# A job order that knows array shapes, one tail tile, an edge copy on VectorE and three FFN slices inside attention

## The chip, the cores and the metric

The kernel runs on one core of a Trainium2 chip. The metric is the device time of one execution in microseconds (us): the median of three runs of the kernel before is 946.44 us (945.19 to 946.77). The engines are named as the profile names them: PE (TensorE, with PEld for its weight loads), DVE (VectorE), ACT (ScalarE), POOL (GpSimd) and SP, the queue that issues DMAs.

## The reference

Windowed attention over 4 batches, 8 heads, 576 positions and head size 64, then two feed-forward layers (FFN) over the 2304 tokens. The weights arrive as 64-bit floats, which is why they have to be taken apart on the chip.

```
scores = (q @ k.T) / 8, plus slope[h] * -|i - j|;  kept where 0 <= i - j < 128
attn   = exp(scores - rowmax) / (rowsum + 1e-9);   x = (attn @ v) as 2304 x 512
h = x @ w_in;  g = h * sigmoid(1.702 * h);         x = g @ w_out     # 512 -> 2048 -> 512
h = x @ w_in2; g = h if h >= 1, 0 if h <= -1, else (h + 1)**2 / 4;   out = g @ w_out2
```

## The kernel before

**Attention** is cut into 16 units (a batch and a pair of heads). For each unit: SP loads q, k and v; PE transposes q and k in three steps (job q, line 339; step 2 is the tail of 64 positions) and DVE or ACT copies them out of PSUM (qe); PE forms scores in three groups (s, line 359); DVE adds the bias and takes the row maximum (t, line 370); ACT takes exp (x, line 378); DVE inverts the row sums (n1, n2); POOL scales (po, line 394); PE transposes the five blocks of probabilities (pt, line 406) and ACT copies all five out (pe, line 411); PE multiplies with v (pv, line 429), and ACT and DVE copy the two result tiles into the FFN's input xt (x0 and x1, lines 438 and 441).

**Weights.** The FFN has 16 slices of 128 hidden units. A slice comes as two raw halves (its part of w_in, then of w_out), each one DMA of 512 KB into one of two raw buffers. Each half passes seven steps: ACT Abs (line 197), four on DVE (199, 202, 205, 208), ACT cast to the high part (211), and the low part (213; on POOL within attention, on DVE later). A raw buffer is free after line 208.

**The order** of the attention part is written out by a planner: `jobs` lists every step with an engine, a cost, its needs, its buffers and a key, `in_order` walks the engines' queues with these costs, and the kernel issues the jobs as it returns them. The engines run in that order. SPLIT = 4 slices (8 halves) are converted among the attention jobs, and the first token block's input is split into high and low parts there (xh, xl).

**FFN.** Tokens go in 5 blocks of about 461. For a step i, stage h (12 matmuls of slice f, line 497) is followed by the activation (ACT 503, DVE 504, ACT 510, DVE 511) and, LAG = 2 steps later, by stage o (12 matmuls, line 558). A run is a block with a range of slices: block 0 with slices 0 to 7 (CUT = 8), block 1 with all 16, block 0 again with 8 to 15, then blocks 2 to 4. While the first runs work, the other 12 slices are converted, one every W1_PACE = 1.6 steps. After the first run its four sums are put aside: DVE copies each to `part` (line 522), which uses the two `ga` buffers of the activation, and SP writes it to DRAM (523). The second FFN is like the first, with blocks of 384. From line 475 on, Tile's own scheduler sets the order.

Of the kernel before, what the change touches and what calls it, by code (L numbers as in the profile page):

```python
# [30 lines left out]
KEYS = dict(dma=-3.04, v=-0.71, b=-0.56, q=-0.6, qe=-0.52, s=-0.5, t=-0.3, x=0.08, n=0.67, po=-0.49, pt=0.98, pe=0.72, pv=0.29, xe=0.54)  # L31
STEP, QSTEP, W_AT, W_STEP, XS_AT = 0.243, 0.09, 3.72, 1.69, 28.0
NM = 5
RUNS = [(0, 1), (2, 3), (4,)]
SHAPE_SWITCH, SLACK, AHEAD = 95, 150, 12
# [6 lines left out]
def jobs(nu, n_heads2, halves, chunks):  # L42
# [8 lines left out]
    for u in range(nu):  # L51
        def at(what, x=0.0):
            return u + KEYS[what] + x

# [6 lines left out]
        for c in range(3):  # L61
            occ, lat = (433, 631) if c < 2 else (114, 314)
            add(("q", u, c), "PE", occ, lat, at("q", c * QSTEP), [("dma", u), ("ident",)] + [("q", u, 0)] * (c > 0),
                [("a", (u, c))] + [("qk", u)] * (c == 0), [("raw", u)] * (c == 2), "128x128")
            occ, lat = (600, 725) if c < 2 else (157, 290)
            add(("qe", u, c), "DVE" if c < 2 else "ACT", occ, lat, at("qe", c * QSTEP), [("q", u, c)], gives=[("a", (u, c))])
        for g, ms in enumerate(RUNS):
            occ = (486, 648, 162)[g]
            banks = [("s", (u, g, e)) for e in range(len(query_groups(ms[0])))]
            add(("s", u, g), "PE", occ, occ + 195, at("s", g * STEP), [("qe", u, c) for c in range(g + 1)],  # L70
                banks + [("p", (u, m)) for m in ms], [("qk", u)] * (g == 2), "64x64")
            done = []
            for m in ms:
                for e, i, lo in query_groups(m):
                    k = {64: 0, 128: 1, 192: 2}[192 - lo]
                    x = g * STEP + 0.01 * (2 * m + e)
                    needs = [("s", u, g)] + [("b", u % n_heads2, e)]
                    add(("t", u, g, m, e), "DVE", (145, 212, 277)[k], (262, 329, 394)[k], at("t", x), needs,
                        gives=banks[e:e + 1] * (m == ms[-1]))
                    add(("x", u, g, m, e), "ACT", (343, 385, 439)[k], (472, 514, 568)[k], at("x", x), [("t", u, g, m, e)])  # L80
                    done.append(("x", u, g, m, e))
            add(("n1", u, g), "DVE", 73, 204, at("n", g * STEP), done)
            add(("n2", u, g), "DVE", 90, 340, at("n", g * STEP), [("n1", u, g)])
            for m in ms:
# [7 lines left out]
                add(("pt", u, m), "PE", 325 if wide else 217, 523 if wide else 415, at("pt", m * STEP / 2),
                    needs + [("pt", u, 0)] * (m > 0),
                    [("t", (u, m))] + [("pt", u)] * (m == 0), [("p", (u, m))], "128x128")
                add(("pe", u, m), "ACT", 365 if wide else 260, 510 if wide else 400, at("pe", m * STEP / 2),
                    [("pt", u, m)], gives=[("t", (u, m))])
        add(("pv", u), "PE", 1400, 1600, at("pv"), [("dmav", u)] + [("pe", u, m) for m in range(NM)],
            [("a", (u, 3)), ("a", (u, 4))], [("pt", u), ("v", u)], "64x64")
        add(("x0", u), "ACT", 306, 450, at("xe"), [("pv", u)], gives=[("a", (u, 3))])
        add(("x1", u), "DVE", 391, 500, at("xe"), [("pv", u)], gives=[("a", (u, 4))])  # L100
    for h in range(halves):
        key = W_AT + W_STEP * h
        add(("wd", h), "SP", 600, 4300, key - 1.0, takes=[("wraw", h)])
        for i, (eng, occ, lat) in enumerate((
                ("ACT", 590, 740), ("DVE", 343, 560), ("DVE", 343, 530), ("DVE", 604, 800), ("DVE", 600, 800),
# [542 lines left out]
```

## Time and profile before

| | |
|---|---|
| median of three runs | 946.44 us (945.19 to 946.77) |
| the profiled execution's own time | 945.34 us |
| its span, first to last instruction | 943.6 us |
| PE, PEld busy | 921.8 us (98%), 810.7 us (86%) |
| DVE, ACT, POOL busy | 546.8, 398.2, 76.7 us |
| granted TensorE clock | 1.000 over the whole span |
| chain that ended last | PE 85%, DVE 6%, DMA 4%, ACT 2% |

The profile's "busy" on PE includes the modelled ends of pipelined matmuls, so two starts of a row of the timeline tell more of PE's pace than the busy share. The clock column (granted clock 1.000, which is the level of 2.4 GHz) is the same in every stretch, so times of different stretches can be compared as they stand. In the timeline, the first column is the start and the second the duration, both in us; a bracket at the end gives the engine's idle time before the row and what ended it.

### The profile page before, as it was taken

How to read it: one execution, taken by the hardware profiler on the slowest of the kernel's cores; microseconds unless marked ns; L12 is line 12 of the kernel's file. 1: busy time of each engine (PE TensorE's matmuls, PEld its weight loads, DVE VectorE, ACT ScalarE, POOL GpSimd, SP SyncE). 2: the span in 40 equal slices, each digit the busy share in tenths (PEclk: the TensorE clock that was granted, in tenths of full speed). 3: DMA queues.
4: the chain of work that ended last, by engine and by line, in shares of the span. 5: the costliest groups of instructions: out<-in, count | busy, mean ns of one | idle time of the engine just before them, and what ended most of it. 6: DMA issues, size and time to landing. Idle time of an engine off the chain costs nothing.

```text
span 943.6 us, 15391 instructions
## 1 busy us (share of the span) xinstructions
PE 921.8 (98%) x5904; PEld 810.7 (86%) x5904; DVE 546.8 (58%) x1290; ACT 398.2 (42%) x948; POOL 76.7 (8%) x176
## 2 busy tenths in 40 slices
PE   7989989999999999999999999999999999999998
PEld 5667678788888989999888989899899998998997
DVE  6887988999334223322589899634434434344343
ACT  5988984454323213222355455422422323323322
POOL 4555640000000000000000000000000000000000
PEclk9999999999999999999999999999999999999999
DMA  5777524444200000000044244000000000000000
GB/s 131 163 171 181 156 81 130 151 126 145 66 1 1 1 1 1 1 1 0 1 134 134 91 133 134 35 1 1 34 0 1 34 1 1 34 1 1 34 1 33
DMA packets 83129, 55.31 MB, mean 59 GB/s; under 512 B 59120, under 2 KB 76784, under 8 KB 83056
## 3 DMA queue, kind: packets, MB, share of 16 engines
q1 hardware_dynamic: 82912, 54.21, 20.1%
q8 instruction: 46, 0.75, 0.3%
q14 instruction: 27, 0.22, 0.1%
q10 hardware_dynamic: 144, 0.13, 0.0%
HBM read 48.66 MB, written 5.66 MB: 58 GB/s over the span
## 4 chain that ended last, share of the span: by engine, by line
PE 85%; DVE 6%; DMA 4%; ACT 2%; SPq 1%; issue 1%; POOL 0%; ACTq 0%; DVEq 0%; POOLq 0%
PE ph L497 39%; PE o L560 21%; PE o L558 19%; PE ps_x L429 2%; DMA raw<-in_moe_w_in_dram 2%; PE ps_s L359 2%; DMA raw<-in_moe_w_out_dram 1%; PE ps_t L406 1%; PE ps_qk L339 1%; DVE x L208 1%; DVE x L205 1%; DVE p L370 1%; DMA qkraw<-in_k_dram 1%; DVE qk L345 1%; DMA sp<-part 1%
## 5 line engine op out<-in xcount | busy, mean ns | idle before, releaser
L497 PE MATMUL ph<-xs,w 128*128 128x384 f32 (+2 forms) x2112 | 431.2, 353 | 0.0
L497 PEld LDWEIGHTS ph<-xs,w 128*128 128x128 f32 x2112 | 385.2, 188 | 28.6
L558 PE MATMUL o<-gs,w 128*128 128x460 f32 (+1 forms) x960 | 214.5, 372 | 2.3 <-DVE part L522 1.8
L560 PE MATMUL o<-w,gs 128*128 128x512 f32 x864 | 215.8, 394 | 0.0
L558 PEld LDWEIGHTS o<-gs,w 128*128 128x128 f32 x960 | 180.2, 188 | 24.0 <-DVE part L522 2.8
L560 PEld LDWEIGHTS o<-w,gs 128*128 128x128 f32 x864 | 161.2, 188 | 30.0 <-ACT gs L510 0.3
L510 ACT CAST gs<-ph 128x384 fp32r<-128x384 f32 (+2 forms) x176 | 89.4, 508 | 164.3 <-DVE ph L508 111.9
L511 DVE TENSOR_TENSOR gs<-ph,gs 128x384 fp32r<-128x384 f32 (+2 forms) x176 | 104.3, 593 | 71.5 <-ACT gs L510 71.4
L507 DVE TENSOR_TENSOR ph<-ph,ga 128x384 f32<-128x384 f32 x96 | 54.2, 565 | 145.0 <-ACT ga L506 145.0
L504 DVE TENSOR_TENSOR ph<-ph,ga 128x460 f32<-128x460 f32 (+1 forms) x80 | 51.4, 643 | 125.0 <-ACT ga L503 124.9
L506 ACT ACTIVATE ga<-ph,half 128x384 f32<-128x384 f32 x96 | 55.8, 581 | 139.3 <-PE ph L497 133.6
L503 ACT ACTIVATE ga<-ph 128x460 f32<-128x460 f32 (+1 forms) x80 | 44.1, 553 | 138.9 <-PE ph L497 138.6
L394 POOL TENSOR_SCALAR p<-p,sm 128x192 f32<-128x192 f32 (+1 forms) x144 | 61.7, 447 | 41.1 <-DVE sm L370 12.8
L197 ACT ACTIVATE x<-raw 128x512 f32<-128x512 f32 x64 | 43.1, 675 | 47.7 <-DMA raw<-in_moe_w_out_dram 23.2
L378 ACT ACTIVATE p<-p,sm 128x192 f32<-128x192 f32 (+1 forms) x144 | 62.1, 438 | 0.0
L508 DVE SCALAR_TENSOR_TENSOR ph<-ga,ph 128x384 f32<-128x384 f32 x96 | 53.8, 561 | 2.8
L211 ACT CAST w<-x 128x512 fp32r<-128x512 f32 x64 | 39.5, 619 | 20.9 <-DVE x L208 19.7
L370 DVE CUSTOM_DVE_ANT_0 p<-ps_s,bias 128x192 f32<-128x192 f32 (+1 forms) x144 | 41.7, 331 | 9.0 <-PE ps_s L359 8.1
L205 DVE SCALAR_TENSOR_TENSOR x<-raw,x 128x512 int32<-128x512 int32 x64 | 44.0, 688 | 0.5
L208 DVE SCALAR_TENSOR_TENSOR x<-raw,x 128x512 int32<-128x512 int32 x64 | 43.8, 686 | 0.7
L406 PE MATMUL ps_t<-ident,p 128*128 128x128 f32 x208 | 36.7, 288 | 5.5 <-POOL p L394 3.9
L213 DVE TENSOR_TENSOR w<-x,w 128x512 fp32r<-128x512 f32 x56 | 38.3, 687 | 2.2 <-ACT w L211 0.6
(47 smaller groups left out, 468.3 us busy)
## 6 DMA issues: line engine op xcount, KB each, us to landing
raw<-in_moe_w_in_dram SPq DMA_DIRECT2D x32, 512.0 KB, 3.7
raw<-in_moe_w_out_dram SPq DMA_DIRECT2D x32, 512.0 KB, 3.5
out_dram<-ob SPq DMA_DIRECT2D x17, 256.0 KB, 2.0
vraw<-in_v_dram SPq DMA_DIRECT2D x32, 128.0 KB, 2.9
qkraw<-in_q_dram SPq DMA_DIRECT2D x30, 128.0 KB, 3.9
qkraw<-in_k_dram SPq DMA_DIRECT2D x30, 128.0 KB, 2.7
sp<-part SPq DMA_DIRECT2D x4, 231.0 KB, 4.3
xt<-sp SPq DMA_DIRECT2D x4, 231.0 KB, 2.9
```

Source lines behind the costliest of these rows:

```text
L205: nc.vector.scalar_tensor_tensor(out=x, in0=raw[:, :, 0], scalar=29, in1=x, op0=ALU.logical_shift_right, op1=ALU.bitwise_or)
L208: nc.vector.scalar_tensor_tensor(out=x, in0=raw[:, :, 1], scalar=SIGN_TOP, in1=x, op0=ALU.bitwise_and, op1=ALU.bitwise_or)
L378: nc.scalar.activation(x, x, AF.Exp, bias=sm[:, 0, a, e:e + 1], scale=-1.0, accum_out=sm[:, 1, a, e:e + 1])
L394: nc.gpsimd.tensor_scalar(out=x, in0=x, scalar1=st[u]["sm", g][:, 2, a, e:e + 1], scalar2=1.0, op0=ALU.mult, op1=ALU.mult)
L497: nc.tensor.matmul(ph, w[f][:, a, 0, c * P:(c + 1) * P], xs[r][c][:, b, :], start=(c == 0 and i == 0), stop=(c == KC - 1 and i == 2))
L506: nc.scalar.activation(a, ph, AF.Relu, scale=0.5, bias=half)
L507: nc.vector.tensor_tensor(out=ph, in0=ph, in1=a, op=ALU.max)
L508: nc.vector.scalar_tensor_tensor(out=ph, in0=a, scalar=1.0, in1=ph, op0=ALU.min, op1=ALU.mult)
L510: nc.scalar.copy(gs[:, 0, :], ph)
L511: act_last[0] = nc.vector.tensor_tensor(out=gs[:, 1, :], in0=ph, in1=f32(gs[:, 0, :]), op=ALU.subtract)
L558: nc.tensor.matmul(o[r][m][:, 0:n], w[f][:, a, 1, sl], gs[:, b, :], start=first, stop=last)
L560: nc.tensor.matmul(o[r][m], gs[:, b, sl], w[f][:, a, 1, :], start=first, stop=last)
```

## The change

- The planner's PE shapes are now "square" (128 x 128: q, pt, and the new h) and "half" (s, pv), with a cost of its own for each pair of neighbours (SWITCH), where before any change of shape cost 95. Costs of s and pv are raised, and every kind of job has new keys, for each step its own.
- The 64-row tails of q and k lie in one raw tile (q on partitions 0 to 63, k on 64 to 127), so that one 128 x 128 transpose takes the place of two of 64 rows.
- Of the two edge blocks of probabilities (m = 0 and 4), the copy of m = 4 goes to DVE; ACT keeps four of five.
- SPLIT = 5: ten halves are converted within attention. CUT = 5: the first run has slices 0 to 4, and the third 5 to 15. The conversion of the other 11 slices starts at step 2, one every 1.5 steps.
- Stage h of slices 0 to 2 for block 0 and its activation (jobs h, ga, gm, gc, gl) are part of the planner's order, in the PSUM banks of the scores. In `stage_h` these three steps then issue nothing. The sigmoid waits for the last unit's last exp.
- The four `part` copies go to ACT. The split of block 0's input is planned from chunk 3 to chunk 0.

```diff
-SPLIT = 4
-CUT = 8
+SPLIT = 5
+CUT = 5
+AHEAD_H = 3
 LAG = 2
-W1_PACE, W2_PACE = 1.6, 1.66
+W1_PACE, W2_PACE = 1.5, 1.66
...
-KEYS = dict(dma=-3.04, v=-0.71, b=-0.56, q=-0.6, qe=-0.52, s=-0.5, t=-0.3, x=0.08, n=0.67, po=-0.49, pt=0.98, pe=0.72, pv=0.29, xe=0.54)
+KEYS = dict(
+    dma=(14.11,), v=(17.92,), b=(-9.64,), q=(-5.39, -6.79, -5.67), qe=(-0.81, 1.92, 1.52), s=(-5.08, -4.22,
...
+EDGE = ("ACT", "DVE")
...
-SHAPE_SWITCH, SLACK, AHEAD = 95, 150, 12
+SWITCH = {("square", "square"): 57, ("square", "half"): 105, ("half", "square"): 140, ("half", "half"): 10}
+SLACK, AHEAD = 52, 12
...
+                eng = "ACT" if wide else EDGE[m > 0]
+                occ, lat = (365, 510) if wide else (260, 400) if eng == "ACT" else (391, 500)
+                add(("pe", u, m), eng, occ, lat, at("pe", m), [("pt", u, m)], gives=[("t", (u, m))])
...
+    for f in range(AHEAD_H):
+        key = KEYS["h"][0] + KEYS["h"][1] * f
+        add(("h", f), "PE", 2510, 2700, key, [("xl", c) for c in range(chunks)] + [("w6", 2 * f)], [("s", ("h", f))],
+            shape="square")
+        if f <= LAG:
+            last = [("x", nu - 1, g, m, e) for g, ms in enumerate(RUNS) for m in ms for e, _, _ in query_groups(m)]
+            needs = [("h", f)] + (last if f == 0 else [("ga", f - 1)])
+            add(("ga", f), "ACT", 450 + 1300 * (f == 0), 600 + 1300 * (f == 0), key + KEYS["h"][2], needs)
...
-                if j.shape and shape and j.shape != shape:
-                    t = max(t, clock[eng] + SHAPE_SWITCH)
+                if j.shape and shape:
+                    t = max(t, clock[eng] + SWITCH[shape, j.shape])
...
-            n = 256 if c < 2 else 64
-            for i in range(2):
-                for t in range(0, n, P):
-                    r = min(P, n)
-                    nc.tensor.transpose(
-                        ps[:, i, t:t + r], d["raw"][0:r, i, 2 * c + t // P].rearrange("p h d -> p (h d)"),
-                        ident[0:r, 0:r])
+            for i, t in [(i, t) for i in range(2) for t in range(2)] if c < 2 else [(0, 0)]:
+                x = d["raw"][:, 4 * i + 2 * c + t if c < 2 else 8]
+                nc.tensor.transpose(ps[:, i, t * P:(t + 1) * P], x.rearrange("p h d -> p (h d)"), ident)
...
+        def do_h(f):
+            h_psum[f] = ps_s.tile([P, 512], F32, tag="s", name="ph")[:, 0:B1[0]]
+            products_h(h_psum[f], w1[f], xs0)
+            ahead[f] = (h_psum[f], None)
...
+            if (which, r) == (1, 0) and f in ahead:
+                ph, gs = ahead[f]
+                if gs is not None:
+                    gt[r, f] = gs
+                    return
...
-                    nc.vector.tensor_copy(part, src[:, 0:n])
+                    nc.scalar.copy(part, src[:, 0:n])
...
-    W1_AT = {max(0, round((g - SPLIT) * W1_PACE)): g for g in range(SPLIT, NF)}
+    W1_AT = {LAG + round((g - SPLIT) * W1_PACE): g for g in range(SPLIT, NF)}
```

**Place 1: PE within attention.** In these rows `ps_qk` is a q or k transpose, `ps_s` a score, `ps_t` the transpose of a probability block (`p_105` to `p_114` are its ten buffers before) and `ps_x` the product with v; xN counts repeats. This is the kernel before, some four units in.

```order
L406 MATMUL ps_t<-ident,p_110 128x128 x2
L339 MATMUL ps_qk<-ident,qkraw 128x128 x4
L359 MATMUL ps_s<-qk 64x192 x2
L406 MATMUL ps_t<-ident,p_111 128x128 x3
L406 MATMUL ps_t<-ident,p_112 128x128 x3
L339 MATMUL ps_qk<-ident,qkraw 128x128 x4
L406 MATMUL ps_t<-ident,p_113 128x128 x3
L406 MATMUL ps_t<-ident,p_114 128x128 x2
L359 MATMUL ps_s<-qk 64x64 x2
L359 MATMUL ps_s<-qk 64x128 x2
L359 MATMUL ps_s<-qk 64x192 x4
L429 MATMUL ps_x<-pt,vraw 64x64 x32
```

And this is one unit of the changed kernel in the same part (its p buffers are `p_108` to `p_117`), from the product with v to the scores ahead of the next one.

```order
L472 MATMUL ps_x<-pt,vraw 64x64 x32
L401 MATMUL ps_s<-qk 64x192 x8
L448 MATMUL ps_t<-ident,p_113 128x128 x2
L448 MATMUL ps_t<-ident,p_111 128x128 x3
L381 MATMUL ps_qk<-ident,qkraw 128x128 x4
L448 MATMUL ps_t<-ident,p_114 128x128 x3
L381 MATMUL ps_qk<-ident,qkraw 128x128 x4
L448 MATMUL ps_t<-ident,p_115 128x128 x3
L381 MATMUL ps_qk<-ident,qkraw 128x128
L448 MATMUL ps_t<-ident,p_117 128x128 x2
L401 MATMUL ps_s<-qk 64x192 x2
L401 MATMUL ps_s<-qk 64x64 x2
```

Before, no two units have the same sequence, and scores stand among the transposes; now the sequence repeats unit after unit, with all transposes in one stretch, and the scores of a unit stand about two products with v ahead of its own transposes.

**Place 2: ACT where attention ends.** `ga_2761` and `gs_2760` are the activation of slice 3, `x_2730` and `x_2739` the two halves of slice 5, `x_2825` the first half of slice 6 (each reads a raw buffer that a DMA fills), and `xs_2767` to `xs_2776` the high parts of block 1's input. The changed kernel:

```order
L234 CAST w_2577<-x_2673 128x512
L220 ACTIVATE x_2730<-raw_2728 128x512
L265 ACTIVATE ga_2761<-ph_2747 128x462
L220 ACTIVATE x_2739<-raw_2737 128x512
L234 CAST w_2727<-x_2730 128x512
L575 CAST gs_2760<-ph_2747 128x462
L279 CAST xs_2767<-xt0_67 128x460
L279 CAST xs_2770<-xt1_68 128x460
L220 ACTIVATE x_2825<-raw_2823 128x512
L234 CAST w_2727<-x_2739 128x512
L279 CAST xs_2773<-xt2_69 128x460
L279 CAST xs_2776<-xt3_70 128x460
```

Block 1's input is now split right behind the attention, with three waits for weight DMAs among its casts; before, that split stands eight steps of the FFN in.

**Place 3: the four sums of the first run.** Before, their copies (`part_3068` to `part_3086`) stand in DVE's order:

```order
L208 SCALAR_TENSOR_TENSOR x_3037<-raw_3035,x_3037 128x512
L522 COPY part_3068<-o0_2727 128x462
L511 TENSOR_TENSOR gs_3058<-ph_3045,gs_3058 128x460
L522 COPY part_3074<-o1_2728 128x462
L213 TENSOR_TENSOR w_3025<-x_3037,w_3025 128x512
```

In the changed kernel they stand in ACT's:

```order
L587 COPY part_2917<-o0_2711 128x462
L575 CAST gs_2907<-ph_2894 128x460
L220 ACTIVATE x_2886<-raw_2884 128x512
L234 CAST w_2874<-x_2877 128x512
L587 COPY part_2923<-o1_2712 128x462
L587 COPY part_2929<-o2_2713 128x462
L234 CAST w_2874<-x_2886 128x512
L220 ACTIVATE x_2941<-raw_2939 128x512
L587 COPY part_2935<-o3_2714 128x462
L265 ACTIVATE ga_2972<-ph_2958 128x460
```

Between the first and the second copy ACT now has an Abs that reads a raw buffer and a cast that needs DVE's four steps; the third copy and the next sigmoid share the two `ga` buffers with the copies, as before.

## Rows read from the trace of the kernel before

**Rows 1.** Busy time by stretch; columns: window, length, busy by engine, clock, DMA.
```profile
0.00:131.54 131.54, 115.73 (x1969) 85.26 (x1969) 104.82 (x494) 111.13 (x421) 76.13 (x176) 1.00 0.63 149
139.20:200.00 60.80, 58.55 (x276) 51.43 (x275) 55.20 (x104) 30.71 (x57) 0.00 (x0) 1.00 0.43 133
200.00:943.60 743.60, 739.89 (x3627) 667.06 (x3625) 379.35 (x682) 250.47 (x462) 0.00 (x0) 1.00 0.11 36
```
**Rows 2.** PE's timeline, from three places within attention and from its end.
```profile
18.84 0.77 PE L359 MATMUL ps_s<-qk 64*64 64x64 f32 x16
19.54 1.81 PE L429 MATMUL ps_x<-pt,vraw 128*64 128x64 f32 x61
21.14 0.37 PE L359 MATMUL ps_s<-qk 64*64 64x192 f32 x1
...
85.72 1.43 PE L359 MATMUL ps_s<-qk 64*64 64x64 f32 x32
87.07 0.44 PE L406 MATMUL ps_t<-ident,p 128*128 128x128 f32 x2
...
110.65 0.60 PE L339 MATMUL ps_qk<-ident,qkraw 128*128 128x128 f32 x4
111.18 0.54 PE L359 MATMUL ps_s<-qk 64*64 64x192 f32 x4
111.66 0.87 PE L406 MATMUL ps_t<-ident,p 128*128 128x128 f32 x6
112.37 0.60 PE L339 MATMUL ps_qk<-ident,qkraw 128*128 128x128 f32 x4
...
129.72 1.89 PE L429 MATMUL ps_x<-pt,vraw 128*64 128x64 f32 x64
131.54 7.82 PE L497 MATMUL ph<-xs,w 128*128 128x462 f32 x36
139.20 2.64 PE L558 MATMUL o<-gs,w 128*128 128x462 f32 x12
```
**Rows 3.** The chain that ended last, at 59 and at 68 us: start, us, what.
```profile
59.34 4.28 DMA raw<-in_moe_w_in_dram
...
68.88 4.36 DMA raw<-in_moe_w_out_dram
```
**Rows 4.** ACT busy from 10 us to the end of attention.
```profile
10.00:131.54 121.54, 109.69 (x420) 1.00 0.64 153
```
**Rows 5.** ACT's groups by shape within attention: busy us, mean ns, idle before.
```profile
L411 ACT COPY pt<-ps_t 128x256 f32<-128x256 f32 x32 | 12.0, 374 | 0.9 <-PE ps_t L406 0.7
...
L197 ACT ACTIVATE x<-raw 128x512 f32<-128x512 f32 x9 | 6.1, 678 | 3.0 <-DMA raw<-in_moe_w_in_dram 2.2 <-DMA raw<-in_moe_w_out_dram 0.7
...
L211 ACT CAST w<-x 128x512 fp32r<-128x512 f32 x8 | 5.0, 620 | 0.0
```
**Rows 6.** Timeline of ACT and DVE where attention ends.
```profile
131.65 0.43 ACT L438 COPY xt<-ps_x 128x320 f32<-128x320 f32 x1 [0.21 <-PE ps_x L429]
...
133.09 0.41 DVE L441 COPY xt<-ps_x 128x256 f32<-128x256 f32 x1
...
134.78 1.28 ACT L503 ACT_TABLE_LOAD   x1
136.07 0.56 ACT L503 ACTIVATE ga<-ph 128x462 f32<-128x462 f32 x1
```
**Rows 7.** SP's issues of the w_in halves of slices 5 and 15.
```profile
134.17 0.37 SPq L190 DMA_DIRECT2D raw<-in_moe_w_in_dram  x1
...
217.95 0.38 SPq L190 DMA_DIRECT2D raw<-in_moe_w_in_dram  x1
```
**Rows 8.** The first run's sums put aside: DVE's first and third copy.
```profile
179.76 0.63 DVE L522 COPY part<-o 128x462 f32<-128x462 f32 x1
...
184.77 0.64 DVE L522 COPY part<-o 128x462 f32<-128x462 f32 x1 [0.23 <-DMA sp<-part]
```
**Rows 9.** DMA issues from 134 to 240 us: count, size, median us to landing.
```profile
raw<-in_moe_w_in_dram SPq DMA_DIRECT2D x13, 512.0 KB, 3.7
...
sp<-part SPq DMA_DIRECT2D x4, 231.0 KB, 4.3
```

More of the change, by code (lines that the diff above doesn't have):

```diff
@@ L51, in jobs, with at @@
     for u in range(nu):
-        def at(what, x=0.0):
-            return u + KEYS[what] + x
+        def at(what, i=0, x=0.0):
+            return u + KEYS[what][i] + x
         n = 14 if u == 0 else 6
@@ L93, in jobs @@
                     needs + [("pt", u, 0)] * (m > 0),
[L94 to L99, printed above, removed]
@@ L100, in jobs @@
-        add(("x1", u), "DVE", 391, 500, at("xe"), [("pv", u)], gives=[("a", (u, 4))])
-    for h in range(halves):
[L102 to L105, printed above, removed]
-                ("ACT", 515, 730), ("POOL", 1254, 1400))):
-            add((f"w{i}", h), eng, occ, lat, key + 0.01 * i, [(f"w{i - 1}", h)] if i else [("wd", h)],
+                    [("t", (u, m))] + [("pt", u)] * (m == 0), [("p", (u, m))], "square")
@@ new lines, in jobs @@
+                eng = "ACT" if wide else EDGE[m > 0]
+                occ, lat = (365, 510) if wide else (260, 400) if eng == "ACT" else (391, 500)
+                add(("pe", u, m), eng, occ, lat, at("pe", m), [("pt", u, m)], gives=[("t", (u, m))])
+        add(("pv", u), "PE", 1600, 1840, at("pv"), [("dmav", u)] + [("pe", u, m) for m in range(NM)],
+            [("a", (u, 3)), ("a", (u, 4))], [("pt", u), ("v", u)], "half")
+        add(("x0", u), "ACT", 306, 450, at("xe", 0), [("pv", u)], gives=[("a", (u, 3))])
@@ L108, in jobs @@
+        add(("x1", u), "DVE", 391, 500, at("xe", 1), [("pv", u)], gives=[("a", (u, 4))])
+    for h in range(halves):
+        key = KEYS["half"][0] + KEYS["half"][1] * h
+        add(("wd", h), "SP", 600, 4300, key + KEYS["wd"][0], takes=[("wraw", h)])
+        for i, eng in enumerate(W_ENG):
+            occ, lat = W_COST[eng, i]
+            add((f"w{i}", h), eng, occ, lat, key + KEYS["w"][i], [(f"w{i - 1}", h)] if i else [("wd", h)],
                 [("wx", h)] * (i == 0), [("wraw", h)] * (i == 4) + [("wx", h)] * (i == 6))
@@ L230, in tile_window_attention_two_ffn, with products_h, sigmoid, new_g @@
     NX = max(B1 + B2)
+    g_p = ctx.enter_context(tc.tile_pool(name="g_p", bufs=2))
+    def products_h(ph, w, xs):
+        for c in range(KC):
+            for i, (a, b) in enumerate(((0, 0), (0, 1), (1, 0))):
+                nc.tensor.matmul(
+                    ph, w[:, a, 0, c * P:(c + 1) * P], xs[c][:, b, :],
+                    start=(c == 0 and i == 0), stop=(c == KC - 1 and i == 2))
+    def sigmoid(ph, n):
+        a = g_p.tile([P, 512], F32, tag="ga", name="ga")[:, 0:n]
+        nc.scalar.activation(a, ph, AF.Sigmoid, scale=1.702)
+        return a
+    def new_g(n):
+        return g_p.tile([P, 2, NX], F32R, tag="gs", name="gs", bufs=LAG + 1)[:, :, 0:n]
+    def low_g(gs, ph):
+        return nc.vector.tensor_tensor(out=gs[:, 1, :], in0=ph, in1=f32(gs[:, 0, :]), op=ALU.subtract)
     def split_block(t0, n):
@@ L240, in split_block @@
         return parts
+    ahead = {}
     with ExitStack() as actx:
@@ L304, in do_dma @@
             d = st[u]
[L305 removed]
+            d["raw"] = raw_p.tile([P, 9, 2, D], F32, tag="raw", name="qkraw")
             c0 = 2 if u == 0 else 0
@@ L410, in do_pe @@
             c = chunks_of(m)
-            nc.scalar.copy(d["pt"][:, 3 * m + c[0]:3 * m + c[-1] + 1, :], d["ps_t", m][:, c[0]:c[-1] + 1, :])
+            copy = nc.vector.tensor_copy if m in (0, NM - 1) and EDGE[m > 0] == "DVE" else nc.scalar.copy
+            copy(d["pt"][:, 3 * m + c[0]:3 * m + c[-1] + 1, :], d["ps_t", m][:, c[0]:c[-1] + 1, :])
         def do_pv(u):
```

97 lines of the change are left out of this document (58 added, 39 removed).

## The prediction

> **What bounds the kernel now.** I read the stretches first. From 200 us on PE is busy 739.89 of 743.60 us and has the same work after the change, so only what lies ahead can move [rows 1]. In the attention, up to 131.54 us, no engine is full: PE 115.7, ACT 111.1, DVE 104.8 [rows 1]. From 139.20, where stage o of slice 0 starts, to 200 PE loses 2.25 us, all near the end of the first run [rows 1, 8]. The granted clock is 1.00 throughout.
>
> Next PE's own pace. From the first product with v (19.54) to the last (129.72) are 15 units in 110.2 us, 7.35 us each [rows 2]. The pieces of a unit, from start to next start where nothing waits [rows 2]: two q steps 2 x 0.53 (110.65 to 111.18); 13 probability transposes at 0.71 / 6 = 0.118, so 1.54 (111.66 to 112.37); a tail transpose 0.12; the small score group 0.48 (111.18 to 111.66); the two large ones 1.35 (85.72 to 87.07); the product 1.60 (19.54 to 21.14). With a change of shape between scores and product (the product takes 1.82 into full-array work at 129.72, 1.60 into scores, so 0.2) that is 6.35 us. The last three units lack the q and s of units that no longer exist, about 3 x 3.0. So PE needs some 15 x 6.4 - 9 = 87 us of the 110, and waits about 20. The chain shows two of the causes: at 59.34 and 68.88 the attention stands behind weight DMAs of 4.28 and 4.36 us, because ACT's Abs of a half whose data had not landed holds everything behind it [rows 3].
>
> So the attention is bound by waits in orders that don't fit, not by an engine, and the rest by PE alone. The figure to work out is T, the time at which stage o of slice 0 starts: 139.20 before, behind three stages h of 7.66 us together (131.54 to 139.20) [rows 2].
>
> **The attention.** The new order repeats one sequence per unit. Scores stand two products ahead of their own transposes, some 12 us for a way through DVE, ACT and POOL that needs about half of it; the weight DMAs are issued early. The first product comes later: ahead of it now stand 13 more transposes (1.54), a unit's q (1.18) and two score groups (0.48 + 0.70), so 19.54 + 3.9 = 23.4. Then 15 x 6.35 - 9 + 7.66, since stages h of slices 0 to 2 stand where the missing units' work was: 94 us, last product at 117.4, its end 1.8 later. Stage o writes the banks of that product's results, so it waits for their copies, 0.43 on ACT behind a pause of 0.21 and 0.41 on DVE [rows 6], about 0.7: T = 119.9 if nothing else waits.
>
> ACT gives a second floor. After 10 us it works 109.69 of 121.54 us [rows 4]. It loses 16 edge copies of 0.374 (-6.0), gains Abs and cast of two more halves, 2 x (0.678 + 0.620) = 2.6 [rows 5], and the activation of three slices with the table load, 6 x 0.56 + 1.28 = 4.6 [rows 6]: 110.9, so 120.9 if it never idles, of which some 2.5 us (slice 4) come after T. If it idles the same 11.9 us as before, T is 130.3. DVE gains 16 copies of 0.41 (6.6 us, hidden only while DVE is not the bound), two halves and six activation steps on its 104.8, so it gets close too.
>
> T lies between 119.9 and 130.3. I take 123, nearer the floor: three of the twenty us of waits stay, because three engines over 90% busy leave no room for a late step, but the two visible causes go. The tail tile itself gives 16 x 0.12, about 2 us of PE, which is in these numbers; its DMAs keep their count. The three stages h cost nothing extra as long as the last three units have that hole.
>
> On the shapes, the rows say that scores take 0.70 us into a product (18.84 to 19.54), as if a change lay there, while the new cost table counts both as "half" at 0.01. The Trainium skill (TensorEngine Tiling (Array Packing), Tiling Modes) says that a change of tiling mode drains the array, and lists 128 x 64 and 64 x 64 as two modes; the product stands at 128*64 and the scores at 64*64 [rows 2], so by the rule, too, the planner misses one change per unit, 16 x 0.2 = 3 us that its order does not avoid. The trace agrees; without that change T would be 3 us lower, and the sum goes by the row.
>
> **The FFN from T on.** The same matmuls as before from 139.20 on, 804.4 us, but with other waits. Before they are 2.3 us. Now:
> - Block 1's input is split right behind the attention, and ACT must first pass three Abs that wait for weight DMAs; the third stands between the casts. If slice 5's first DMA goes out at T + 1.5, when slice 4 frees its buffer, landing (3.7 [rows 9]), Abs and DVE's steps bring slice 6's landing to about T + 12.7, and the third cast to T + 14.5; PE wants it at T + 13.8 (five stages of 2.55 and half of the next). With the low parts 1.0, bounds 0 and 4.
> - The first run's sums: before, DVE copied at 179.76 the first and at 184.77 the third, which had to wait for the first one's DMA of about 4.3 us, as both use two buffers [rows 8, 9]. ACT has the same two buffers, and between first and second copy an Abs and a cast that depend on DMA and DVE. PE needs all four banks for the next block. I take 3.4 instead of 2.3: bounds 1 (ACT copies at once) and 6 (a DMA and a half's DVE steps more).
> - The last slices: before, 83.8 us lay between the w_in issues of slices 5 and 15 [rows 7], 8.4 each, with DVE 91% busy, and PE needed slice 15 some 20 us later than it was ready. Now it is ready at T + 1.5 + 83.8 + 8 = T + 93.3 (8 is 3.7 to land, 0.68, 0.62 and DVE's steps), and its stage h comes after 35 stages of 2.55, at T + 89, plus the waits above, T + 94. No margin is left: 1.4, bounds 0 and 8. The split for the third run falls into the same busy stretch: 1.2, bounds 0 and 2.
>
> Together 7.0 against 2.3: +4.7. Later nothing differs: the conversion of the second FFN's weights is paced as before.
>
> **Sum**, against the profiled execution's 945.34: -(139.20 - 123.0) = -16.2, +4.7, so 933.8. The median of the runs lay 1.1 above the profiled one; I add it: 934.9. With the bounds of T and of the waits (T from 119.9 to 127, waits from +1 to +8) the likeliest case itself spans 928 to 942.
>
> **Rivals.**
> 1. The waits stay: the new order is full in PE, ACT and DVE at once, and each late step is handed on. ACT then idles as before, T = 130.3: 945.34 - 8.9 + 4.7 + 1.1 = 942.2; with the 20 us of PE's waits kept, T = 137 and 949. For it: ACT and DVE come near 100% in T = 123, and 16 DVE copies add to that. Against it: scores lead by two units, and the edge copies leave ACT. 15%.
> 2. Slower than before: conversion starves PE in the second run. Three slices are now loaded in steps 4, 5 and 6 in a row, beside the split and the put-aside sums, and ACT's order waits at each Abs. If a slice then takes 10.5 us instead of 8.4, slice 15 is ready at T + 114.5, 20 us after PE wants it: 934.9 + 19 = 954. It decides from about 9.7 us a slice on, where the late 13 us eat the gain. For it: DVE's 91%. Against it: 8.4 already contains a put-aside and a split. 5%.
> 3. The FFN's new waits don't come (ACT is less busy than DVE was there, and the spare steps before slices are needed cover them): T = 121, 945.34 - 18.2 + 0.5 + 1.1 = 928.7, or less. 10%.
>
> **How the numbers follow.** Forecast 70%, rivals 15, 5 and 10%. The range 928.5 to 942.5 leaves out the upper half of rival 1, rival 2 and the lower part of rival 3. What a measurement of this kernel can tell from no change is 0.2%, 1.9 us. Faster by more: the forecast, rival 3, most of rival 1 and a little of 2, 93%; within: 3%; slower: 4%.
>
> **What would show it.** In the changed profile: products with v 6.2 to 6.6 us apart without a break, no weight DMA on the chain before 115 us, three groups of 12 stage-h matmuls between the last three products; stage o of slice 0 at 120 to 127; then PE waits of some 1 us at block 1's first stage h, 2 to 4 around the part copies and 1 to 3 at slices 14 and 15, and none from the third run's second step on. T beyond 129 would show rival 1 right, PE waits on `w` of 10 us or more rival 2. I would be wrong altogether if the gain came from after 300 us, or if stage h shifted the products of the last units by its whole length.

## The result, and the profile after

The changed kernel takes 936.77 us (median of four runs, 935.74 to 937.98); the kernel before, beside it, 945.82. The ratio is 0.9907, 95% interval 0.9885 to 0.9929. The predicted 934.9 is 1.9 us below the measured time. A second series gave 938.46 and a ratio of 0.9916 (0.9901 to 0.9931). The profiled execution took 937.98 us, with a span of 936.2.

The stretches of the changed kernel, as in [rows 1] (window, length, busy PE, PEld, DVE, ACT, POOL, granted clock, DMA share, GB/s), split where stage o of slice 0 starts:

```profile
0.00:128.59 128.59, 111.84 (x1989) 91.02 (x1989) 108.62 (x516) 109.37 (x412) 78.16 (x176) 1.00 0.65 154
128.59:200.00 71.41, 69.68 (x323) 61.63 (x324) 63.61 (x115) 35.82 (x67) 2.78 (x2) 0.98 0.43 139
200.00:936.20 736.20, 730.72 (x3579) 657.37 (x3577) 372.58 (x671) 246.78 (x457) 0.00 (x0) 1.00 0.11 35
```

Stage o of slice 0 starts at T = 128.59 instead of 139.20 [rows 2]: 10.6 us earlier. From there to the end it is 807.6 us instead of 804.4, so 3.2 are given back: 945.34 - 10.6 + 3.2 is the measured 937.9. The clock is no longer 1.00 throughout.

PE's timeline of the changed kernel, which answers to [rows 2]: the first product and the twelfth, then the end of the attention, where the three stages h (L259, 12 matmuls each) stand between the last products:

```profile
23.89 1.81 PE L472 MATMUL ps_x<-pt,vraw 128*64 128x64 f32 x61
...
98.34 1.81 PE L472 MATMUL ps_x<-pt,vraw 128*64 128x64 f32 x61
...
109.20 2.77 PE L259 MATMUL ph<-xs,w 128*128 128x462 f32 x12
...
114.78 2.77 PE L259 MATMUL ph<-xs,w 128*128 128x462 f32 x12
...
120.47 2.77 PE L259 MATMUL ph<-xs,w 128*128 128x462 f32 x12
123.17 0.34 PE L472 MATMUL ps_x<-pt,vraw 128*64 128x64 f32 x4
124.01 1.76 PE L472 MATMUL ps_x<-pt,vraw 128*64 128x64 f32 x60 [0.51 <-ACT xt L481]
128.59 4.10 PE L623 MATMUL o<-gs,w 128*128 128x462 f32 x12 [2.81 <-DVE xt L484]
132.52 1.84 PE L259 MATMUL ph<-xs,w 128*128 128x462 f32 x8
```

Where nothing waits, products are 6.2 to 6.4 apart, but the eleven units from 23.89 to 98.34 average 6.77. The difference is in PE's waits from 14 us to the end of the attention (us in total, times, longest):

```profile
PE ps_qk L381 <- DMA qkraw<-in_k_dram: 6.3, 5, 1.8
PE o L623 <- DVE xt L484: 2.8, 1, 2.8
PE ps_x L472 <- ACT xt L481: 0.5, 1, 0.5
PE ps_t L448 <- ACT pt L454: 0.2, 1, 0.2
```

PE now waits for loads of k. SP, which issues all loads in order, goes at the same pace: from unit to unit its first load of q comes 6.75 us later (ten units lie between these two rows of its timeline).

```profile
21.11 1.07 SPq L359 DMA_DIRECT2D qkraw<-in_q_dram  x2
...
88.61 1.15 SPq L359 DMA_DIRECT2D qkraw<-in_q_dram  x2
```

At the seam, where the attention hands over to the FFN, the timeline of DVE, and under it that of POOL, in the changed kernel, while PE stands idle from 125.8 (124.01 + 1.76) on:

```profile
125.68 0.41 DVE L222 TENSOR_SCALAR x<-x 128x512 f32<-128x512 f32 x1
126.12 1.44 DVE L225 TENSOR_SCALAR x<-x 128x512 int32<-128x512 int32 x1
127.48 0.62 DVE L272 TENSOR_TENSOR gs<-ph,gs 128x462 fp32r<-128x462 f32 x1
128.03 0.41 DVE L484 COPY xt<-ps_x 128x256 f32<-128x256 f32 x1
```
```profile
126.01 1.26 POOL L236 TENSOR_TENSOR w<-x,w 128x512 fp32r<-128x512 f32 x1 [3.05 <-ACT w L234]
```

The copy x1 of the last unit (L484), whose PSUM bank stage o needs, stands behind two conversion steps of slice 4 and a step of the activation (L272), and one of the conversion steps took 1.44 us beside POOL's step instead of 0.43. PE's clock around this pause (window, length, PE busy, clock, DMA):

```profile
126.00:128.50 2.50, 0.00 (x0) 0.93 0.54 195
128.50:131.00 2.50, 2.41 (x6) 0.50 0.00 0
...
132.00:133.00 1.00, 1.00 (x7) 1.00 1.02 358
```

The first stage o runs at half clock (granted clock 0.50), 3.93 us (128.59 to 132.52) instead of some 2.55: 1.4 us. The waits after it, and SP's issues of the w_in halves of slices 5 and 15 (the row that answers to [rows 7]):

```profile
144.76 1.32 PE L259 MATMUL ph<-xs,w 128*128 128x460 f32 x5 [0.32 <-DVE xs L280]
157.97 2.60 PE L623 MATMUL o<-gs,w 128*128 128x460 f32 x10 [1.41 <-ACT part L587]
227.15 0.89 PE L259 MATMUL ph<-xs,w 128*128 128x462 f32 x3 [0.65 <-DVE xs L280]
228.30 1.95 PE L259 MATMUL ph<-xs,w 128*128 128x462 f32 x8 [0.26 <-DVE xs L280]
```
```profile
130.26 0.37 SPq L213 DMA_DIRECT2D raw<-in_moe_w_in_dram  x1
...
212.21 0.38 SPq L213 DMA_DIRECT2D raw<-in_moe_w_in_dram  x1
```

### The profile page after: what moved, and what is told of

Its sections match the earlier page's. It is cut to its first block, busy times and chain, and to the rows that moved or that the text cites. A ratio compares the mean times of both kernels' runs of the same rounds, so it can differ in the third digit from the quotient of the medians.

```text
span 936.2 us, 15327 instructions
## 1 busy us (share of the span) xinstructions
PE 912.2 (97%) x5888; PEld 810.0 (87%) x5888; DVE 544.8 (58%) x1300; ACT 392.0 (42%) x936; POOL 80.9 (9%) x178
## 4 chain that ended last, share of the span: by engine, by line
PE 71%; DMA 10%; DVE 8%; ACT 5%; SPq 3%; issue 2%; POOL 0%; ACTq 0%; DVEq 0%; POOLq 0%
PE ph L259 34%; PE o L625 21%; PE o L623 13%; DMA raw<-in_moe_w_in_dram 4%; DMA raw<-in_moe_w_out_dram 3%; DMA qkraw<-in_k_dram 2%; DVE x L228 2%; DVE x L231 2%; ACT x L220 2%; SPq L359 2%; ACT p L420 1%; PE ps_x L472 1%; DVE w L236 1%; DVE x L222 1%; DVE gs L272 1%
## 5 line engine op out<-in xcount | busy, mean ns | idle before, releaser
L259 PE MATMUL ph<-xs,w 128*128 128x384 f32 (+2 forms) x2112 | 432.3, 353 | 1.3 <-DVE xs L280 1.2
L259 PEld LDWEIGHTS ph<-xs,w 128*128 128x128 f32 x2112 | 384.2, 188 | 31.6 <-DVE xs L280 2.3
L272 DVE TENSOR_TENSOR gs<-ph,gs 128x384 fp32r<-128x384 f32 (+2 forms) x176 | 104.4, 593 | 71.6 <-ACT gs L575 71.4
L568 DVE TENSOR_TENSOR ph<-ph,ga 128x460 f32<-128x460 f32 (+1 forms) x77 | 49.5, 643 | 125.5 <-ACT ga L265 125.5
L228 DVE SCALAR_TENSOR_TENSOR x<-raw,x 128x512 int32<-128x512 int32 x64 | 45.6, 714 | 0.5
L231 DVE SCALAR_TENSOR_TENSOR x<-raw,x 128x512 int32<-128x512 int32 x64 | 44.7, 700 | 0.7
L381 PE MATMUL ps_qk<-ident,qkraw 128*128 128x128 f32 x144 | 26.3, 288 | 12.5 <-DMA qkraw<-in_k_dram 7.7
```

Of the source, the lines that this page charges most:

```text
L228: nc.vector.scalar_tensor_tensor(out=x, in0=raw[:, :, 0], scalar=29, in1=x, op0=ALU.logical_shift_right, op1=ALU.bitwise_or)
L231: nc.vector.scalar_tensor_tensor(out=x, in0=raw[:, :, 1], scalar=SIGN_TOP, in1=x, op0=ALU.bitwise_and, op1=ALU.bitwise_or)
L259: nc.tensor.matmul(ph, w[:, a, 0, c * P:(c + 1) * P], xs[c][:, b, :], start=(c == 0 and i == 0), stop=(c == KC - 1 and i == 2))
L272: return nc.vector.tensor_tensor(out=gs[:, 1, :], in0=ph, in1=f32(gs[:, 0, :]), op=ALU.subtract)
```

## The experiments

Each ratio is to the kernel before, timed in the same series (medians 945.10 to 945.82). T and the last column are of each kernel's profiled execution, and T alone says little: it was 128.59 and 130.53 in two profiles of the changed kernel. In the second one PE waited longer for a load of k, and ran at half clock behind it, in the middle of the attention (timeline; then window, length, PE busy, PEld, DVE, ACT, POOL, clock, DMA):

```profile
103.78 0.66 PE L381 MATMUL ps_qk<-ident,qkraw 128*128 128x128 f32 x2 [2.07 <-DMA qkraw<-in_k_dram]
...
104.00:106.50 2.50, 2.50 (x12) 2.17 (x11) 1.46 (x6) 0.48 (x1) 0.74 (x2) 0.50 0.69 158
```

The profiles of the order alone, of stage h outside and of the edge copies on ACT have such a half clock too, from 102.9 or 105.0 us on; the changed kernel's first profile and all others have none within the attention. No row of the table down to the fourth v buffer can be told from the changed kernel by its time; the interval of the x copies first still overlaps both of the changed kernel's.

| kernel | median us | ratio to before (interval) | T | span - T |
|---|---|---|---|---|
| before | 945.82 | | 139.20 | 804.4 |
| changed | 936.77 | 0.9907 (0.9885 to 0.9929) | 128.59 | 807.6 |
| changed, again | 938.46 | 0.9916 (0.9901 to 0.9931) | 130.53 | 808.8 |
| order alone | 936.61 | 0.9904 (0.9887 to 0.9920) | 130.13 | 805.0 |
| stage h outside | 936.98 | 0.9903 (0.9886 to 0.9920) | 130.58 | 807.3 |
| put-aside copies on DVE | 937.36 | 0.9913 (0.9895 to 0.9931) | 126.76 | 805.9 |
| edge copies on ACT | 936.15 | 0.9901 (0.9885 to 0.9918) | 128.59 | 808.9 |
| more shape changes | 937.41 | 0.9919 (0.9902 to 0.9936) | 128.28 | 807.4 |
| fourth v buffer | 937.92 | 0.9916 (0.9900 to 0.9933) | 127.15 | 808.3 |
| x copies first | 940.36 | 0.9942 (0.9925 to 0.9959) | 127.10 | 812.5 |
| both of these | 941.92 | 0.9959 (0.9940 to 0.9978) | 123.81 | 811.0 |
| x first, casts before slice 6 | 937.76 | 0.9919 (0.9905 to 0.9933) | 124.57 | 809.8 |
| and before half of slice 5 | 940.00 | 0.9944 (0.9929 to 0.9959) | 127.51 | 810.6 |
| and low parts on POOL | 949.02 | 1.0032 (1.0018 to 1.0046) | 125.52 | 819.0 |

**The order alone.** The new order stays, with the tail tile and the edge copy on DVE. After planning, jobs of slice 4 and of stage h are left out of the list, and the FFN is that of before (cut lines are marked by three dots):

```diff
-SPLIT = 5
-CUT = 5
+SPLIT = 4
+CUT = 8
...
-W1_PACE, W2_PACE = 1.5, 1.66
+W1_PACE, W2_PACE = 1.6, 1.66
...
+            for _, (what, *args) in in_order(jobs(NU, NP, 10, KC), CAPS):
+                later = what in ("h", "ga", "gm", "gc", "gl") or what[0] == "w" and args[-1] >= 2 * SPLIT
+                if not later:
+                    do[what](*args)
...
-                    nc.scalar.copy(part, src[:, 0:n])
+                    nc.vector.tensor_copy(part, src[:, 0:n])
...
-    W1_AT = {LAG + round((g - SPLIT) * W1_PACE): g for g in range(SPLIT, NF)}
+    W1_AT = {max(0, round((g - SPLIT) * W1_PACE)): g for g in range(SPLIT, NF)}
```

> The new order of attention, the tail tile and the edge copy stay; the FFN is that of before (four slices converted inside, first run to slice 7, steps at 1.6, put-aside copies on DVE, stage h outside). The order of the jobs that remain is the changed kernel's. Theory: the order and the tail tile carry the gain, since the new places of stage h, of slice 4 and of the cut only shift work between two places: the last product starts 2 to 6 us ahead of the changed kernel's 124.0, three stages h of 7.7 us follow, stage o starts at 127 to 130, the FFN takes 804 to 806, and the time is 934 to 938. Rival: the stages h inside fill holes that stay empty here; then the last product stays at 124, stage o starts at 133.5, and the time is 940 to 942.

936.61 us: the whole gain, from the order with its tail tile (the edge copy, taken back below, is worth nothing that shows). T is 130.13, 9.1 us ahead of before, and the FFN takes 805.0, close to the 804.4 of before. The expected way failed in part: the last product stayed at 123.81. The scheduler of the FFN's code put 15 of the 36 stage-h matmuls between the last products by itself:

```profile
115.87 0.69 PE L259 MATMUL ph<-xs,w 128*128 128x462 f32 x2
116.53 0.46 PE L259 MATMUL ph<-xs,w 128*128 128x462 f32 x1
117.08 1.93 PE L259 MATMUL ph<-xs,w 128*128 128x462 f32 x8
119.59 1.88 PE L472 MATMUL ps_x<-pt,vraw 128*64 128x64 f32 x64
121.92 1.08 PE L259 MATMUL ph<-xs,w 128*128 128x462 f32 x4
123.81 1.88 PE L472 MATMUL ps_x<-pt,vraw 128*64 128x64 f32 x64 [0.80 <-DVE xt L484]
125.62 4.67 PE L259 MATMUL ph<-xs,w 128*128 128x462 f32 x21
```

**Stage h outside**, all else as changed (the jobs h, ga, gm, gc, gl are skipped):

```diff
+                if what not in ("h", "ga", "gm", "gc", "gl"):
+                    do[what](*args)
```

> The three stages h of block 0 and their activation are taken out of the attention's order and run right behind it, all else in the same order. Theory of the prediction: they fill holes that the last units leave, so the last product stays near 123.2, its end at 125, then 7.7 us of stage h and the sigmoid with its table load: stage o at 133 or later, 4 to 5 us slower than with them inside (941). Rival: PE had no holes there, the last product moves forward by the whole 7.7 us to about 115.6, stage o starts at 125 to 128.6 and the time is the same or up to 3 us lower.

The rival holds: the time is the same. Here too 15 matmuls slipped in, and the last product started at 124.24, against 124.01 with all 36 inside. But this profile has the half clock at 105 us, and so it is better compared with the changed kernel's second one: there the last product starts at 125.78, 1.5 us later. So, by these two profiles, the attention's holes hide about 3 of the 4.5 us that the 21 other matmuls take. T gains nothing (130.58 and 130.53), because the pause of 2.80 us at the seam is missing when stages h stand there.

**Two more parts, undone.** The put-aside copies on DVE, and the last probability block's copy on ACT, each in its old place of the order:

```diff
-                    nc.scalar.copy(part, src[:, 0:n])
+                    nc.vector.tensor_copy(part, src[:, 0:n])
```

> Only the four put-aside copies go back to DVE. Theory: they wait for buffers, the third for the first one's DMA, on either engine, so PE waits 1 to 2.5 us there as now (1.4), and the time is within 1.5 us of the changed kernel (936.8). Rival: DVE, which converts the weights, is the bound up to 220 us; four copies of 0.63 more on it delay slice 15 and the split for the third run by 2.5 us, and the time rises by 2 to 3 us (939).

```diff
-            copy = nc.vector.tensor_copy if m in (0, NM - 1) and EDGE[m > 0] == "DVE" else nc.scalar.copy
+            copy = nc.scalar.copy
```

> Only the copy of the last probability block of each unit goes back from DVE to ACT, in the same place of the order. Theory of the prediction: ACT, 109.4 us busy of the 128.6 before stage o of slice 0, is a floor; with 6.0 us more it is at 115.4, its idle time of 19 us covers part, and stage o starts 2 to 4 us later: 939 to 940. Rival: PE and the loads set the pace in the attention, ACT has room, and the time changes by less than 1 us.

Neither changes the time. On DVE the four sums cost three pauses of 0.84, 0.96 and 0.62, on ACT one of 1.41. With the edges on ACT it works 112.84 us up to 128.59 instead of 109.37, and T is the same 128.59: ACT is no floor.

**More changes of shape** (PE's order alone):

```diff
+            for u in range(2, NU):
+                i = todo.index(("s", u, 1))
+                n = next(j for j in range(i + 1, len(todo)) if todo[j][0] in ("s", "pv", "h", "pt"))
+                if todo[n][0] == "pt":
+                    todo.insert(n, todo.pop(i))
```

> In PE's order alone, the second score group of a unit moves behind the two probability transposes and the q step that follow it, or behind the next transpose job: changes between full-array work and the half-array work (scores, products) go from 39 to 65 in the attention (81 before the change). Theory: the change gained its time in PE's busy time by avoiding such changes. PE was busy 115.7 us up to the end of the attention before and 104.2 after without the stages h, 11.5 less, of which 1.9 are the tail tile; 9.6 over 42 changes are 0.23 each. So 26 changes cost 6.0 us of PE and the time rises by 4 to 6 us, to 941 to 943. Rival: the time went down because waits went; then the 6 us of waits for k data take up the extra changes, and the time rises by less than 1.5 us.

The rival holds: 937.41, T 128.28. PE's waits for k data after 14 us are 0.18, 0.80, 0.26, 0.65 and 0.62, 2.5 us instead of 6.3. PE did more and waited less. So PE is not what sets the pace of a unit any more. The price of a change still shows in PE's own time: from 14 us to T, less PE's waits, it is 107.6 us here, and 104.2 to 105.6 in the eight profiles with 39 changes, stage h inside and no half clock in the attention. That makes 2.0 to 3.5 us for 26 changes, 0.08 to 0.13 each (an estimate), and not the 0.23 of the theory.

**A fourth v buffer:**

```diff
-        v_p = pool("v_p", CAPS["v"])
+        v_p = pool("v_p", CAPS["v"] + 1)
```

> Theory: PE's waits for k data in the attention (after 20 us: 0.57, 1.52, 1.59, 1.83 and 0.78, 6.3 us together) come from SP's queue: a load of v that waits for one of three v buffers holds the loads of q and k behind it; a unit takes SP 6.8 us, of which its issues alone are about 5.9. With a fourth v buffer and the same order these waits fall below 2 us, stage o of slice 0 starts near 124, and the time falls by about 4 to 5 us (932). Rival 1: SP is full by its issues, or the transfers themselves are slow: the waits stay at about 6 us and the time is the same. Rival 2: k comes earlier, but ACT or DVE is the next bound: the waits move to ps_t and ps_x, and the time falls by under 1.5 us.

No gain that can be told from the spread of T. The waits for k fell from 6.3 to 3.9 (3.5 to 8.0 us in the other kernels with this order), and SP, held less by v buffers, now waited for q and k buffers. Which of SP's issue time, the buffers and the transfers sets the 6.75 us is open.

**The x copies first**, and then with the fourth v buffer too ("both"):

```diff
+            for name, ahead_of in ((("x0", NU - 1), ("gc", 1)), (("x1", NU - 1), ("w1", 8))):
+                todo.remove(name)
+                todo.insert(todo.index(ahead_of), name)
```

> Theory: the pause of 2.81 us ahead of stage o of slice 0 comes from DVE's order, in which the copy x1 of the last unit stands behind two weight steps of slice 4, and the granted clock of 0.50 behind it comes from that pause. Then, with x0 and x1 of the last unit ahead of those steps, stage o starts at about 126.4 instead of 128.59 with a pause under 1 us, the clock stays near 1.00, the first stage o takes 2.6 us instead of 3.9, and the time falls by 3 to 4 us (933). Rival 1: the copy is only the last of several late things (the low part gl of slice 0, the copy on ACT), and the start stays past 128: no change. Rival 2: the start is earlier, but slice 4's conversion is now later and the splits and the last slices give half of it back: 935.

> Theory: the two causes are independent, so the gains add: 8 us, about 929, with stage o of slice 0 at 121 to 122. Rival: the conversion of the later slices (DVE and the two raw buffers) sets the end of the second run; then an earlier start turns into waits on w at slices 13 to 15 and at the split for the third run, and only 4 to 5 us remain (932).

The seam does what was expected, the time does not: 940.36. PE's timeline of the first:

```profile
127.10 2.77 PE L627 MATMUL o<-gs,w 128*128 128x462 f32 x12 [0.54 <-ACT xt L481]
...
144.76 0.75 PE L259 MATMUL ph<-xs,w 128*128 128x460 f32 x1 [4.82 <-ACT xs L279]
145.85 4.37 PE L259 MATMUL ph<-xs,w 128*128 128x460 f32 x11 [0.34 <-DVE xs L280]
...
163.29 2.51 PE L627 MATMUL o<-gs,w 128*128 128x460 f32 x6 [1.75 <-ACT part L591]
```

Pause and half clock at the seam are gone. But the FFN's code is ordered by a scheduler, which answered two moved copies with another order of ACT: the Abs of slice 6, which waits for a DMA, now stands ahead of all four casts of block 1's input and not of two, and the sigmoid of slice 3 (135.24 in the changed kernel) now stands behind the second Abs of slice 5, at 140.01. PE waits 4.82 us there and again runs at half clock behind it. With both edits T is 123.81, near the 123 of the prediction (121 to 122 was expected of this run), and the same pause (4.92) follows. That kernel's twelve runs go from 936.5 to 946.4, and the profile shows the lowest. The granted clock over the whole span is 0.996 in that run and 0.991 in the two slowest, so they ran longer at half clock; where isn't seen.

**The casts moved back**, with the x copies first: ahead of slice 6, and then ahead of the second half of slice 5 too (the second kernel's edit, in part; the first has only the condition on slice 6):

```diff
+            with tc.issue_after(last_cast[0].ins) if g == SPLIT + 1 else nullcontext():
+                load_weights(w1_in, w1_out, g, w1[g], (0,) if g == SPLIT else (0, 1))
+        if i == LAG + 1:
+            with tc.issue_after(last_cast[0].ins):
+                load_weights(w1_in, w1_out, SPLIT, w1[SPLIT], (1,))
```

> The copies x0 and x1 first, as in the first experiment, and ACT's steps of slice 6 behind the four casts of block 1's input. Theory: the first experiment lost at that split what it won at the seam, 4.8 us of pause and some 2 us of half clock behind it, because ACT's order of the FFN had changed with the moved copies and the Abs of slice 6 stood ahead of all four casts. Then that pause falls to 1 to 2 us, the clock stays near 1.00 there, and the time is 933 to 935. Rival: conversion is the bound up to 220 us; then slice 6 and all after it come later, and the time lost at the split appears as waits on w at slices 13 to 15 or at the split for the third run: 937 to 940.

> As the casts-ahead-of-slice-6 kernel, and the second half of slice 5 also behind the four casts of block 1's input, so that they no longer stand behind its Abs, which waited 2.7 us for a DMA. There the pause ahead of block 1 was 4.1 us, and the half clock behind it cost some 2.5 more. Theory: up to 220 us two things must end together, PE's steps and the conversion of eleven slices, which DVE (90% busy) paces at 7.7 to 8 us a slice. Then the pause falls to 1 to 2 us, but PE comes 4 to 6 us earlier to slices 13 to 15, whose weights come no earlier, and waits on w there: 935.5 to 937.5. Rival: the pauses and the clock were the loss, and conversion has slack: no waits on w over 1 us, and 931 to 933.

The first leaves a pause of 4.10, because the casts still stood behind an Abs of slice 5 and the steps of slice 3's activation. So the Abs of slice 6 made only about 0.7 of the 4.82, and my reading of the first experiment was wrong in the main. The second shortens the pause to 2.38, and PE's timeline shows where the rest goes:

```profile
142.69 0.47 PE L259 MATMUL ph<-xs,w 128*128 128x460 f32 x1 [2.38 <-ACT xs L279]
...
160.85 1.40 PE L629 MATMUL o<-gs,w 128*128 128x460 f32 x5 [2.30 <-ACT part L593]
162.04 4.18 PE L259 MATMUL ph<-xs,w 128*128 128x460 f32 x12
...
224.44 3.08 PE L259 MATMUL ph<-xs,w 128*128 128x460 f32 x12 [0.67 <-ACT w L234]
```

The put-aside sums cost 3.1 us (0.77 and 2.30) and a half clock, and after all of it PE still waits for the cast of slice 15. Of the waits on w only 1.1 us came (0.67 and, on PE's weight loads, 0.43), not the 4 to 6 that I expected, since PE lost the time before it got there. But there is no slack: from slice 5's first issue to slice 15's are 82 us in the changed kernel and 84 here.

**Low parts on POOL**, for the eleven slices of the FFN, on top of the kernel just described (940.00):

```diff
-            late.append(partial(convert, 6, raw, x, w, i, nc.vector))
+            late.append(partial(convert, 6, raw, x, w, i, nc.gpsimd if w_in is w1_in else nc.vector))
```

> The kernel before, with the low parts (L236) of slices 5 to 15 on POOL instead of DVE: 22 steps of 0.69 us leave DVE, 15 us of some 85. Theory 1, DVE paces the conversion: it gets faster by 1 us a slice, waits on w go, and the time is 930 to 933. Theory 2, from the seam, where a DVE step that ran beside POOL's 1.26 us took 1.44 instead of 0.43, 1.67 instead of 0.68: each POOL step costs DVE 0.5 to 1.0 us, as much as it takes off; the time stays within 1 us of the kernel without it or is up to 5 us longer.

949.02, which is 9.0 us more than without this edit and slower than before the change: theory 2, and more than its 5 us. Groups of DVE and POOL between 165 and 215 us (busy, mean ns), first without and then with the low parts on POOL:

```profile
L228 DVE SCALAR_TENSOR_TENSOR x<-raw,x 128x512 int32<-128x512 int32 x13 | 8.9, 687 | 0.2
...
L222 DVE TENSOR_SCALAR x<-x 128x512 f32<-128x512 f32 x12 | 5.1, 423 | 2.4 <-ACT x L220 2.4
```
```profile
L236 POOL TENSOR_TENSOR w<-x,w 128x512 fp32r<-128x512 f32 x12 | 16.6, 1380 | 33.6 <-ACT w L234 33.6
L228 DVE SCALAR_TENSOR_TENSOR x<-raw,x 128x512 int32<-128x512 int32 x12 | 16.0, 1335 | 0.3
...
L222 DVE TENSOR_SCALAR x<-x 128x512 f32<-128x512 f32 x12 | 7.6, 636 | 3.3 <-ACT x L220 3.2
```

A half loses a step of 0.686 us on DVE, and two others grow by 0.65 and 0.21: more than it saved. (The other two of its four steps stay as they were: L231 686 and 683, L225 423 and 427 ns.) Conversion of slices 5 to 15 takes 86.7 us (129.61 to 216.28), and PE then waits at slices 14 and 15 and at the third run's split.

**The changed kernel again:**

> The changed kernel itself, on the same chip as these, for their comparison. If the waits are those of its order, stage o of slice 0 starts at 126.5 to 129 again behind a pause of 2.8 us on the copy x1, with a clock of 0.50 behind it, waits for k data are 4 to 6.5 us, and the median is 936 to 938.

T was 130.53 and the median 938.46, both outside what was expected, behind the same pause (2.80) and half clock at the seam; the wait for k of 2.07 us and the half clock behind it, shown above, came on top.

## Why the prediction was right, and which steps were not

**The time, 934.9: 1.9 us too low, and that close by luck in part.** The sum is built on the profiled execution, forecast at 933.8 and measured at 937.98: T came 5.6 us later than forecast, and the FFN lost 1.5 less. The median then lay 1.2 us below the profiled run, where the prediction had added 1.1.

**That only T and the FFN's first 100 us can move: right.** After 240 us there are only two small new pauses, 0.33 and 0.48 us at 527, where the second FFN's conversion starts.

**PE's own unit, 6.35, and the first product at 23.4: right** (6.2 to 6.4 where nothing waits; 23.89).

**"It waits about 20" of 110 us: wrong, and with it that the attention "is bound by waits".** The view of waits lists 8.0 us for the kernel before between 14 and 125 us, of which these are most:

```profile
PE ps_s L359 <- DVE qk L345: 2.5, 3, 0.9
PE ps_t L406 <- POOL p L394: 2.3, 5, 0.7
PE ps_t L406 <- ACT pt L411: 1.3, 3, 0.6
PE ps_x L429 <- DVE xt L441: 0.9, 2, 0.6
PE ps_qk L339 <- DMA qkraw<-in_k_dram: 0.6, 1, 0.6
```

The rest was time in which PE worked in a costlier order: 81 changes between full-array and half-array work, counted in its order, against 39 now, and two tail transposes a unit. From 14 us to T PE waits 9.6 us before and 9.8 in the changed kernel; without these waits it takes 115.6 and 104.8, which is 10.8 less and about all that T moved (10.6). So the gain is PE's own work; the waits changed their place (for k from 0.6 to 6.3) but not their sum. In part it can be divided, by estimates: 42 changes at 0.08 to 0.13 (the run with more changes) are 3 to 5.5 us. The 32 tail transposes took some 4.5 us, from each start to the next, and 16 full ones at 0.109 take 1.7: at most 2.8 less, as changes of shape are in it. The rest is open, and the tail tile wasn't run alone. The sum for T did not rest on the 20 us: it adds up the pieces of the new order, and takes only the 3 that "stay" from them.

**T = 123: 5.6 us too low.** The sum of the terms was 117.4 for the last product, 1.8 for it, 0.7 for the copies and 3 for waits. Measured: the last product 124.0 and the copies 2.8. Two things were missed. PE waited for loads of k, 6.3 us in place of 3 for all waits, and the view of SP's queue, which I had read for the FFN alone, would have shown how little room there was. And I took the copies' time from [rows 6], without counting what stands ahead of x1 in DVE's order and runs beside POOL there. ACT as a second floor was wrong (the run with edges on ACT). And T missed the 120 to 127 that "What would show it" names; in the second profile it is beyond the 129 that was to show rival 1. One weight DMA, at 65.23 for 4.33 us, is still on the chain within the attention, so of the two visible causes one stayed.

**The FFN's waits, 7.0: nearly right in sum (5.5: 807.6 less 802.1, which is 804.4 without its 2.3 of waits), not in parts.** The put-aside sums cost 1.4 instead of 3.4, the split of block 1's input 0.3 instead of 1.0, the last slices under 0.5 (weight loads of PE that wait 0.46 and 0.43) instead of 1.4, the third run's split 0.9 instead of 1.2. In their place came 1.4 of half clock and 0.8 at 527. The mechanism of the last slices was right: 130.26 is T + 1.7, conversion took 82 us instead of 83.8, and PE met slice 15's weights with no margin. The range given for the waits, +1 to +8, does not follow from the bounds of the four terms: these add up to 1 and 20, so -1.3 to +17.7 against 2.3.

**Rivals.** T and the time lie between the forecast and rival 1, but the waits that "stayed" are new ones. (Its T = 137 should be 139.9: the forecast's floor of 119.9 and the 20 us.) Rival 2's mechanism is real and sits close by: in the kernel with low parts on POOL PE waits 5.8 us from slice 14 to the third run's split, part of what takes it to 949.

Against the forecast's mechanism as a whole: stage h inside, the fifth slice and the earlier cut, half of the change's text, bring nothing that these runs can tell (order alone 936.61, changed 936.77 and 938.46). The first profile of the changed kernel has T 1.5 us ahead of the order alone and an FFN 2.6 longer, but the order alone has the half clock at 103 us, which that profile lacks; the second, which has it too, has T 0.4 later and an FFN 3.8 longer.

## What to carry to other kernels

A view of waits and the time without these waits are two sums: take both before saying what a gain will come from. A start won in one stage is worth what the next stage has in slack: here the four kernels with the x copies first and the low parts on DVE reached stage o 1.1 to 4.8 us earlier than the changed kernel's first profile, and none was faster, because PE then stood at the next block's split and at the put-aside sums, which wait for the conversion's steps on ACT and DVE. Before counting a wait as gone, look at the in-order queue that feeds it (SP's issues per unit against PE's) and at what stands ahead of the releasing step in its engine's order. And where part of the order is a scheduler's, compare the whole order after any edit: two moved copies changed ACT's order 15 us later, and what they had won was lost there.

## What the hardware showed

**PE's clock falls behind short pauses.** From T on, after pauses of 2.67 to 4.92 us (eight of eight in these traces), the next 12 matmuls or so ran at a clock of 0.50, the level of 1.2 GHz: 3.9 to 4.1 us instead of 2.55 behind the five pauses of 2.67 to 2.81, and 5.1 to 5.3 behind the three of 4.10 to 4.92. Between 1.41 and 2.50 it went either way: 1.58, 1.69, 1.72, 2.20, 2.30 and 2.33 were followed by it, 1.41, 1.47, 1.52, 1.67, 2.38 and 2.50 were not, and of three pauses of 1.75 one was. Within the attention, from 14 us on, waits for k of 2.03, 2.07, 2.11 and 2.28 were followed by it, 2.04, 2.18 and all shorter ones were not. So such a pause can cost up to 2.6 us more than its length, and which one does, these rows don't tell.

**DVE and POOL take turns.** The step at 126.12 ended at 127.56, 0.29 after POOL's that began ahead of it, and took 1.44 instead of 0.43. The Trainium skill (SBUF — State Buffer, two separate sides) says that the two share a pair of ports that one instruction holds to its end, for DVE steps with two SBUF inputs or in a two-port mode. The trace agrees for the step with two SBUF inputs: a mean of 1335 instead of 687 ns beside POOL's steps. The one-input steps grew as well (636 instead of 423, and the 1.44 above); whether they run in a two-port mode, no row shows.
